# A list schedule made inside the kernel sets the order of four engines behind the first product; loads of pieces and packs on SyncE's queue

## The chip, the cores and the metric

The kernel runs on one core of a Trainium2 chip. The metric is the device time of one execution in microseconds, the median of several runs. TensorE (PE) multiplies, VectorE (DVE), ScalarE (ACT) and GpSimd (POOL) do the elementwise work, SyncE (SP) only issues DMAs. Each engine works through its own list of instructions in order and waits on semaphores for the others.

## The reference

Attention in 8 heads over 8 sequences of 576 tokens, four heads with a window of 32 keys and four with 32 keys at a distance of 4; then a gated feed-forward layer over all 4608 tokens. Inputs and outputs are float32.

```python
scores = scale * np.matmul(q, k.transpose(0, 1, 3, 2))
scores = np.where(masks[None, :, :, :], scores, -1000000000.0)
attn = softmax(scores)                       # written out in the reference
x = np.matmul(attn, v) -> (4608, 512)
g = x @ w_gate                               # 512 x 1536
silu = g * (1.0 / (1.0 + np.exp(-g)))
return silu * (x @ w_val) @ w_out            # 1536 x 512
```

## The kernel before

**Number format.** The products run in a shorter float format (float32r), so each operand is split in a high part (rounded) and a low part (the rest); three products, high-high, low-high, high-low, stand for one.

**Tokens.** They come in nine chunks of 512 columns. The first three (`NPLAIN`) are computed plainly; the last six in three double chunks by a seven-product scheme (Strassen's) that saves one product in eight. Attention comes in 38 packs: scores, mask and maximum (`shift`), `exps`, a turn by TensorE (`turn_e`), a copy (`keys`), `results`, `norm`, `turn_y`, and `x_copies`, which puts the result in place as high and low part. A pack's steps A, B and C are hung into the feed-forward work by a table of slots (`attend`).

**The ramp.** An item is one 128-row slice f of the hidden layer for one chunk: gate product into bank bg (12 matmuls), tanh (`act_tanh`), `dve_u`, value product into bank bv (12), `dve_h`, `h_hi` (rounding, ACT, L537), `h_lo` (low part, POOL, L542), and one item later the out product into bank bo (12, L549), whose last four matmuls need the low part. The first six items have 256 columns (f = 0, 1, 2 for either half of chunk 0), the others 512; items 6 to 14 are f = 3 to 11 of chunk 0, which is when the weights are needed first.

**Weights.** The 24 units of weights arrive as 64-bit numbers (768 KB each, L234, five raw buffers). Each passes five steps, called E, T, B, H and L in the code (`STAGES`): E (ACT, L244) and T (ACT L265 or DVE L268) bring the halves into place, B (DVE, L275 or L278) joins them, H (ACT, L286) rounds, L (POOL, L290) makes the low part. A raw buffer takes its next load when B is done. Units 2f and 2f+1 serve slice f: the gate product needs 2f, the value product both, the out product 2f+1.

**Pieces.** For the last stage the weights are needed in other combinations. They are written to a scratch tensor in DRAM: plain ones straight from the units (`plain_parts`, 54 writes of 256 KB, L692), sums made on DVE and ACT (`mix_stage`, 72 writes, L735). In the last stage 63 pieces of 512 KB are loaded three times (`ask`, POOL's queue, L764) into a ring of seven; a piece serves 12 matmuls (L836). `h_split` (L826, and L797 on POOL or DVE by turns) splits the hidden tiles there, `out_done` stores results (SP, L886).

**Order.** All engines but SP are ordered by hand (`manual_schedule`): instructions run in the order in which the Python code emits them. `unit_first`, `unit_second` and `unit_third` emit the steps of units 2t+2 and 2t+3 at fixed places of item t; `mixing` spreads the 54 mixing stages from item 11 (`W_ITEMS`) on. SP's DMAs were placed by the framework, those of the pieces tied behind the last weight load or mix write (`issue_after`). Pack loads (L347, L354) are issued on ACT's queue behind the exp of the pack before.

## Time and profile before

| what | value |
|---|---|
| time, median of 3 runs (lowest, highest) | 981.69 us (980.54, 985.24) |
| profiled execution, its time | 981.86 us |
| profiled execution, its span | 979.8 us |
| TensorE busy / its weight loads | 926.6 us (95%) / 754.2 us (77%) |
| DVE / ACT / POOL busy | 661.5 (68%) / 386.1 (39%) / 351.8 us (36%) |
| DMA | 204.8 MB, mean 209 GB/s |
| chain that ended last | 68% TensorE, 11% DVE, 4% issue, 3% POOL |

Matmul times are modelled ends and overlap a little; the distance from start to start is the pace. Names are those of the program with buffer numbers left out: bg, bv and bo are the banks of gate, value and out product, `two` that of attention, at_float, at_float32r and at_int are tiles of those types.

### The profile page before, as it was taken

The page shows a single profiled execution, that of the slowest core. Times are in us where ns is not written, and L with a number is a line of the kernel's source. Part 1 is how long each engine was busy: PE and PEld are TensorE (multiplying, and loading weights), DVE is VectorE, ACT ScalarE, POOL GpSimd, SP SyncE. Part 2 cuts the span into 40 slices and gives each one's busy share as a digit, 9 for nine tenths or more (in the row PEclk, how much of TensorE's full clock was granted, in tenths as well). Part 3 has the DMA queues.
Part 4 walks back from the last instruction along what each step waited for, and adds up shares of the span by engine and source line. Part 5 has one row for each costly group of instructions (what it writes and reads, how often), then busy time and mean ns, then how long its engine had stood idle before and what let it go on. Part 6 is the DMA issues. An engine that isn't in the chain of part 4 may idle for free.

```text
span 979.8 us, 20720 instructions
## 1 busy us (share of the span) xinstructions
PE 926.6 (95%) x8701; PEld 754.2 (77%) x8701; DVE 661.5 (68%) x974; ACT 386.1 (39%) x611; POOL 351.8 (36%) x371
## 2 busy tenths in 40 slices
PE   6576988999999999999999989999999999999998
PEld 4475766888888788788788768888888788888886
DVE  4444654665677768876578994767679965465882
ACT  3445453332323233434334443334344533333352
POOL 2334444212211121332324474233244653334582
PEclk7778999999999999999999999999999999999999
DMA  9546523465546577787777577878765596665573
GB/s 356 186 174 207 176 66 111 161 212 197 197 159 229 183 251 255 249 274 238 218 235 237 171 219 231 279 218 264 252 219 171 168 293 207 193 193 173 179 251 108
DMA packets 73964, 204.78 MB, mean 209 GB/s; under 512 B 7440, under 2 KB 21392, under 8 KB 73872
## 3 DMA queue, kind: packets, MB, share of 16 engines
q0 software_dynamic: 27216, 99.10, 33.5%
q1 hardware_dynamic: 36720, 65.98, 19.1%
q10 hardware_dynamic: 9936, 38.39, 11.3%
q8 instruction: 68, 1.11, 0.5%
q14 instruction: 24, 0.20, 0.1%
HBM read 160.97 MB, written 42.47 MB: 208 GB/s over the span
## 4 chain that ended last, share of the span: by engine, by line
PE 68%; DVE 11%; issue 4%; POOL 3%; ACT 2%; DMA 1%; ACTq 0%; POOLq 0%; DVEq 0%
PE bo L836 26%; PE bg L836 10%; PE bv L836 9%; PE bo L549 6%; PE bg L503 6%; PE bv L503 6%; DVE at_float L797 3%; DVE at_float32r L797 2%; PE two L420 2%; PE two L374 2%; POOL at_float32r L797 1%; PE two L406 1%; POOL at_float32r L290 1%; DMA at_float<-qkb 1%; DVE at_float L397 0%
## 5 line engine op out<-in xcount | busy, mean ns | idle before, releaser
L836 PE MATMUL bo<-at_float32r 128*128 128x512 f32 x1296 | 310.3, 392 | 4.9 <-DVE at_float32r L797 4.6
L836 PEld LDWEIGHTS bo<-at_float32r 128*128 128x128 f32 x1296 | 241.4, 188 | 58.1 <-DVE at_float32r L797 5.9
L764 POOL DMA_DIRECT2D at_float32r<-pieces x189 | 103.7, 549 | 267.3 <-PE bo L836 164.7
L797 DVE TENSOR_TENSOR at_float<-bo,at_float 128x512 f32<-128x512 f32 x168 | 113.5, 687 | 99.9 <-ACT at_float L841 53.5
L503 PE MATMUL bg<-at_float32r,at_float32r 128*128 128x512 f32 (+1 forms) x468 | 119.3, 407 | 16.2 <-ACT at_float32r L286 9.3
L836 PE MATMUL bg<-at_float32r 128*128 128x512 f32 x486 | 130.1, 393 | 1.6 <-DVE at_float32r L797 0.8
L836 PE MATMUL bv<-at_float32r 128*128 128x512 f32 x486 | 128.9, 391 | 0.0
L549 PE MATMUL bo<-at_float32r,at_float32r 128*128 128x512 f32 (+1 forms) x468 | 112.4, 388 | 16.7 <-POOL at_float32r L542 16.7
L542 POOL TENSOR_TENSOR at_float32r<-at_float,at_float32r 128x512 fp32r<-128x512 f32 (+1 forms) x39 | 50.6, 1297 | 206.5 <-PE bo L549 126.9
L797 DVE TENSOR_TENSOR at_float32r<-at_float,at_float32r 128x512 fp32r<-128x512 f32 (+1 forms) x84 | 97.3, 1185 | 39.0 <-ACT at_float32r L826 23.6
L503 PEld LDWEIGHTS bg<-at_float32r,at_float32r 128*128 128x128 f32 x468 | 91.3, 210 | 36.2 <-ACT at_float32r L286 10.0
L549 PEld LDWEIGHTS bo<-at_float32r,at_float32r 128*128 128x128 f32 x468 | 84.9, 195 | 35.9 <-POOL at_float32r L542 18.8
L503 PE MATMUL bv<-at_float32r,at_float32r 128*128 128x512 f32 (+1 forms) x468 | 109.8, 385 | 1.5 <-DVE at_float L532 1.5
L836 PEld LDWEIGHTS bg<-at_float32r 128*128 128x128 f32 x486 | 90.3, 188 | 22.2 <-DVE at_float32r L797 1.7
L836 PEld LDWEIGHTS bv<-at_float32r 128*128 128x128 f32 x486 | 90.7, 188 | 19.4
L826 ACT CAST at_float32r<-at_float 128x512 fp32r<-128x512 f32 x126 | 75.0, 622 | 75.0 <-DVE at_float L797 26.9
L797 POOL TENSOR_TENSOR at_float32r<-at_float,at_float32r 128x512 fp32r<-128x512 f32 x63 | 89.5, 1423 | 36.6 <-ACT at_float32r L826 35.8
L503 PEld LDWEIGHTS bv<-at_float32r,at_float32r 128*128 128x128 f32 x468 | 84.9, 196 | 18.2 <-DVE at_float L532 1.8
L862 ACT ACTIVATE at_float<-at_float 128x512 f32<-128x512 f32 x72 | 45.6, 633 | 92.8 <-DVE at_float L797 92.7
L527 DVE SCALAR_TENSOR_TENSOR at_float<-at_float,bg 128x512 f32<-128x512 f32 (+1 forms) x39 | 25.2, 646 | 71.3 <-ACT at_float L522 71.3
L841 ACT COPY at_float<-bg 128x512 f32<-128x512 f32 x63 | 37.1, 588 | 72.2 <-PE bg L836 72.1
L864 DVE SCALAR_TENSOR_TENSOR at_float<-at_float,at_float 128x512 f32<-128x512 f32 x72 | 54.6, 759 | 11.7 <-ACT at_float L862 11.7
(70 smaller groups left out, 944.5 us busy)
## 6 DMA issues: line engine op xcount, KB each, us to landing
at_float32r<-pieces POOLq DMA_DIRECT2D x189, 512.0 KB, 4.6
pieces<-at_float32r SPq DMA_DIRECT2D x126, 256.0 KB, 3.5
at_float<-qkb ACTq DMA_DIRECT2D x32, 576.0 KB, 5.8
at_float<-vb ACTq DMA_DIRECT2D x34, 520.0 KB, 4.6
at_int<-w SPq DMA_DIRECT2D x19, 768.0 KB, 4.3
out<-at_float SPq DMA_DIRECT2D x36, 256.0 KB, 4.6
at_int<-w SPq DMA_DIRECT2D x10, 384.0 KB, 6.7
at_float<-vb SPq DMA_DIRECT2D x8, 260.0 KB, 5.7
```

What stands on the lines that cost most here:

```text
L374: nc.tensor.matmul(out=two[BQ * j:BQ * j + BQ, i, SA + BU * g:SA + BU * g + BU], lhsT=t[r, q:q + BQ], rhs=t[r, k + 1:k + BK], start=not ma ...
L503: nc.tensor.matmul(out=(bank_g, bank_v)[which][:, it.cols], lhsT=wcol(it.f, o, wl), rhs=(x_lo if xl else x_hi)[it.ci % 2][1 - j // 2][:, j ...
L527: last["h"] = nc.vector.scalar_tensor_tensor(out=t, in0=t, scalar=1.0, in1=bank_g[:, it.cols], op0=ALU.add, op1=ALU.mult)
L542: nc.gpsimd.tensor_tensor(out=hl, in0=it.h[0], in1=it.h[1], op=ALU.subtract)
L549: nc.tensor.matmul(out=bank_o[j][:, it.cols], lhsT=wcol(f, 2 * DM + P * j, low), rhs=x, start=f == it.cols.start == low == 0 and x is hh, ...
L764: nc.gpsimd.dma_start(out=taken[asked], in_=pieces[asked % NPIECE])
L797: engine.tensor_tensor(out=out, in0=a, in1=b, op=op)
L826: nc.scalar.copy(out=o[:, 0], in_=src)
L836: nc.tensor.matmul(out=bank, lhsT=w, rhs=x, start=first and n == 0 and t in FRESH, stop=last and n == len(ops) - 1, skip_group_check=True)
L841: nc.scalar.copy(out=kept[KEPT[t]][r], in_=banks[0][r][:, :CS])
L862: nc.scalar.activation(out=f, in_=g, func=AF.Tanh, scale=0.5)
L864: nc.vector.scalar_tensor_tensor(out=f, in0=f, scalar=1.0, in1=g, op0=ALU.add, op1=ALU.mult)
```

## The change

`Desk` stands between the code and the engines. Up to the first product of the feed-forward layer it passes every call on. From `nc.keep` on it records calls with what they read and write, and `nc.issue` at the end orders all of them by a list schedule: each engine takes, among the instructions whose inputs are ready on a modelled clock, the one with the longest way to the end, or waits a little for a longer one. Costs are a constant and a slope for each engine; DMAs go through one modelled pipe of 373 bytes/ns with 2 us to land. TensorE's instructions keep their written order (`spine`). SP is ordered by hand now too. Loads of pieces and packs go to SP's queue. The steps of the units are emitted at the item that needs them (`units`) and mixing from item 15, but the schedule decides when they are issued. No computation is added or taken away.

```diff
+class Desk:
+    COST = {"vector": (155, 1.035), "scalar": (170, 0.86), "gpsimd": (400, 1.75)}
+    OVERLAP, AFTER = {"vector": 80, "scalar": 80}, {"tensor": 180, "sync": 0}
+    LANDING, RATE = 2000, 373
...
+        for k in range(n - 1, -1, -1):
+            e, _, _, cost, later, _, _ = kept[k]
+            way[k] = cost + later + max((way[m] for m in after[k]), default=0)
+            if e == "tensor":
+                if last is not None:
+                    way[k] = max(way[k], cost + way[last])
+                last = k
...
+        spine = [k for k in range(n) if kept[k][0] == "tensor"][::-1]
...
+        def begin(k):
+            e, _, _, _, _, both, _ = kept[k]
+            return max(free[e], ready[k], lock if both else 0)
+
+        while len(order) < n:
+            best = None
+            if spine and not left[spine[-1]]:
+                best = begin(spine[-1]), spine[-1]
+            now = free["tensor"] + (way[spine[-1]] if spine else 0)
+            for e in self.ENGINES[1:]:
+                x = [(begin(k), -way[k], k) for k in queue[e]]
+                if not x:
+                    continue
+                soon = min(x)
+                take = soon
+                for y in sorted(x, key=lambda y: y[1]):
+                    if y[1] >= soon[1]:
+                        break
+                    if y[0] <= soon[0] or soon[0] + kept[soon[2]][3] > max(y[0], now + y[1]):
+                        take = y
+                        break
+                if best is None or take[0] < best[0]:
+                    best = take[0], take[2]
...
+        for k in order:
+            kept[k][1]()
...
-    nc = tc.nc
+    nc = Desk(tc.nc)
...
-    by_hand = tc.manual_schedule(engines={et.PE, et.DVE, et.Activation, et.Pool})
+    by_hand = tc.manual_schedule(engines={et.PE, et.DVE, et.Activation, et.Pool, et.SP})
...
+    nc.keep(dict(tensor=16000, vector=18000, scalar=18000, gpsimd=18000, sync=8000))
...
-                        load_v(m, later, nc.scalar)
+                        load_v(m, later, nc.sync)
...
-                        load_qk(m + 1, later, nc.scalar)
+                        load_qk(m + 1, later, nc.sync)
...
-            nc.gpsimd.dma_start(out=taken[asked], in_=pieces[asked % NPIECE])
+            nc.sync.dma_start(out=taken[asked].bitcast(F32), in_=pieces[asked % NPIECE])
...
-    W_ITEMS = NF - 1
+    W_ITEMS = HALVED + NF
...
+    def units(t):
+        for u in (2 * t, 2 * t + 1):
+            for c in STAGES:
+                if done[c] == u:
+                    w_one(c)
...
+        if it.ci == 0:
+            units(it.f)
         gv_mm(it, 0)
...
+    nc.issue()
+    by_hand.__exit__(None, None, None)
```

The first place is ACT at the start of the ramp, around unit 2 (raw tile 323, joined in tile 493, in the change 444) and pack 2's exp (tile 140). Before:

```order
L286 CAST at_1536_float32r<-at_776_int_346 128x768
L522 ACTIVATE at_512_float_453<-bg 128x256
L402 ACTIVATE at_512_float_140<-at_512_float_140 128x8x63
L244 ACTIVATE at_1536_int_323<-at_1536_int_323 128x768
L265 ACTIVATE at_1536_int_323<-at_1536_int_323 128x768
L537 CAST at_512_float32r<-at_512_float_453 128x256
L286 CAST at_1536_float32r<-at_776_int_493 128x768
L244 ACTIVATE at_1536_int_326<-at_1536_int_326 128x768
```

The same place in the change (every instruction behind the first product has the line of the recorded call, L239):

```order
L223 CAST at_1536_float32r<-at_776_int_346 128x768
L239 ACTIVATE at_1536_int_323<-at_1536_int_323 128x768 x2
L239 ACTIVATE at_512_float_441<-bg 128x256
L239 CAST at_1536_float32r<-at_776_int_444 128x768
L239 ACTIVATE at_512_float_140<-at_512_float_140 128x8x63
L239 ACTIVATE at_1536_int_326<-at_1536_int_326 128x768
L239 COPY at_512_float_240<-two 128x512
L239 CAST at_512_float32r<-at_512_float_441 128x256
```

E and T of unit 2 have moved ahead of the first tanh, and its H ahead of the exp; the rounding of the hidden tile has moved behind.

The second place is POOL from item 2 to item 4. Low parts of the hidden tile go to tile 10616; the tiles of units 6 to 11 are 29400, 30936, 32472, 34008, 35544 and 37080. Before:

```order
L542 TENSOR_TENSOR at10616_512_float32r_512<-at8568_512_float32_453,at9592_512_float32r_510 128x256
L473 TENSOR_TENSOR at19160_1024_float32r_67<-at7304_512_float32_349,at17112_1024_float32r_63 128x2x4x64
L290 TENSOR_TENSOR at29400_1536_float32r_76<-at53976_776_int32_337,at29400_1536_float32r_76 128x768
L290 TENSOR_TENSOR at30936_1536_float32r_77<-at54752_776_int32_346,at30936_1536_float32r_77 128x768
L290 TENSOR_TENSOR at32472_1536_float32r_78<-at55528_776_int32_493,at32472_1536_float32r_78 128x768
L290 TENSOR_TENSOR at34008_1536_float32r_79<-at53976_776_int32_337,at34008_1536_float32r_79 128x768
L542 TENSOR_TENSOR at10616_512_float32r_512<-at9080_512_float32_539,at10104_512_float32r_644 128x256
```

In the change:

```order
L239 TENSOR_TENSOR at19160_1024_float32r_67<-at7304_512_float32_349,at17112_1024_float32r_63 128x2x4x64
L239 TENSOR_TENSOR at10616_512_float32r_443<-at8568_512_float32_441,at9592_512_float32r_442 128x256
L239 TENSOR_TENSOR at29400_1536_float32r_76<-at53976_776_int32_337,at29400_1536_float32r_76 128x768
L239 TENSOR_TENSOR at30936_1536_float32r_77<-at54752_776_int32_346,at30936_1536_float32r_77 128x768
L239 TENSOR_TENSOR at10616_512_float32r_443<-at9080_512_float32_445,at10104_512_float32r_446 128x256
L239 TENSOR_TENSOR at32472_1536_float32r_78<-at55528_776_int32_444,at32472_1536_float32r_78 128x768
```

The low part of item 3 has two units ahead of it instead of four.

The third place is SP's queue behind the load of unit 6. Before, the loads of units 7 to 23 followed each other with nothing between. In the change (raw tiles 14264, 50904 and 52440 are units 7, 8 and 9; 616 and 1896 are pack 4):

```order
L239 DMA pieces_57<-at20184_1536_float32r_70 128x2x256
L239 DMA at616_1280_float32_119<-qkb 128x1152
L239 DMA at14264_1536_int32_323<-w 128x1536
L239 DMA pieces_57<-at23256_1536_float32r_72 128x2x256
L239 DMA at1896_1040_float32_125<-vb 128x1040
L239 DMA at50904_1536_int32_326<-w 128x1536
L239 DMA pieces_57<-at24792_1536_float32r_73 128x2x256 x2
L239 DMA at52440_1536_int32_333<-w 128x1536
```

Writes of plain pieces and the loads of packs have come between the loads of units.

## Rows read from the trace of the kernel before

**Rows 1.** The page's slices: TensorE's busy tenths in 40 equal slices.
```profile
PE   6576988999999999999999989999999999999998
```

**Rows 2.** Stretches: length, busy us (instructions) of each engine, TensorE's clock, DMA share, GB/s.
```profile
22.00:85.00 63.00, 42.62 (x649) 39.08 (x642) 31.47 (x48) 28.50 (x44) 24.41 (x18) 0.75 0.56 193
85.00:185.00 100.00, 86.51 (x730) 69.21 (x731) 57.91 (x79) 44.44 (x63) 39.86 (x25) 0.95 0.40 135
...
160.00:540.00 380.00, 378.59 (x4104) 306.95 (x4103) 270.01 (x438) 132.97 (x204) 91.17 (x96) 1.00 0.65 217
540.00:600.00 60.00, 54.99 (x361) 43.93 (x360) 50.55 (x58) 28.62 (x48) 36.23 (x37) 1.00 0.66 203
600.00:960.00 360.00, 358.47 (x2739) 293.83 (x2738) 253.19 (x352) 146.91 (x247) 155.71 (x187) 1.00 0.71 219
```

**Rows 3.** TensorE's waits, 20 to 160 us: total, times, longest.
```profile
PE bo L549 <- POOL at_float32r L542: 16.7, 6, 4.4
PE bg L503 <- ACT at_float32r L286: 7.4, 2, 4.3
```

**Rows 4.** TensorE in order of time: start, us, instructions [idle before, releaser].
```profile
30.03 3.04 PE L503 MATMUL bg<-at_float32r,at_float32r 128*128 128x256 f32 x12 [3.12 <-ACT at_float32r L286]
...
37.18 1.58 PE L503 MATMUL bv<-at_float32r,at_float32r 128*128 128x256 f32 x12
...
44.53 2.08 PE L503 MATMUL bg<-at_float32r,at_float32r 128*128 128x256 f32 x8 [4.26 <-ACT at_float32r L286]
...
60.22 0.78 PE L503 MATMUL bg<-at_float32r,at_float32r 128*128 128x256 f32 x4 [3.94 <-ACT at_float32r L471]
...
76.44 1.22 PE L549 MATMUL bo<-at_float32r,at_float32r 128*128 128x256 f32 x4 [4.38 <-POOL at_float32r L542]
77.47 2.76 PE L503 MATMUL bg<-at_float32r,at_float32r 128*128 128x256 f32 x12
...
85.45 2.89 PE L503 MATMUL bg<-at_float32r,at_float32r 128*128 128x512 f32 x12
...
98.14 4.50 PE L503 MATMUL bg<-at_float32r,at_float32r 128*128 128x512 f32 x12
102.48 2.89 PE L503 MATMUL bv<-at_float32r,at_float32r 128*128 128x512 f32 x12
...
184.71 2.96 PE L503 MATMUL bg<-at_float32r,at_float32r 128*128 128x512 f32 x12
```

**Rows 5.** The same view of ACT, DVE and POOL, single instructions.
```profile
25.78 0.89 ACT L244 ACTIVATE at_int<-at_int 128x768 f32<-128x768 f32 x1
...
29.16 0.83 ACT L286 CAST at_float32r<-at_int 128x768 fp32r<-128x768 f32 x1
...
27.46 0.96 DVE L275 SCALAR_TENSOR_TENSOR at_int<-at_int 128x768 int32<-128x768 int32 x1 [2.31 <-ACT at_int L265]
...
140.87 1.93 DVE L278 SCALAR_TENSOR_TENSOR at_int<-at_int 128x768 int32<-128x768 int32 x1
...
75.66 0.73 POOL L542 TENSOR_TENSOR at_float32r<-at_float,at_float32r 128x256 fp32r<-128x256 f32 x1
```

**Rows 6.** DMA rate in 40 slices of 0 to 28 us; its mean, 167.2 to 170.2.
```profile
GB/s 0 0 43 147 398 405 407 369 344 400 404 410 410 401 413 401 373 392 404 396 404 371 386 388 410 382 395 405 405 390 396 399 407 388 426 426 426 418 404 325
...
DMA packets 649, 1.10 MB, mean 367 GB/s; under 512 B 63, under 2 KB 167, under 8 KB 648
```

**Rows 7.** SP's longest wait; POOL's piece loads (page); their landing (page).
```profile
SPq L886 <- DVE at_float L797: 402.6, 24, 137.1
...
L764 POOL DMA_DIRECT2D at_float32r<-pieces x189 | 103.7, 549 | 267.3 <-PE bo L836 164.7
...
at_float32r<-pieces POOLq DMA_DIRECT2D x189, 512.0 KB, 4.6
```

**Rows 8.** TensorE's waits, 165 to 980 us.
```profile
PE bo L836 <- DVE at_float32r L797: 4.6, 3, 2.3
...
PE two L374 <- DMA at_float<-qkb: 0.5, 1, 0.5
```

More of the change, by code (lines that the diff above doesn't have):

```diff
@@ L166, in attention_moe @@
     assert M_RAW + 2 * WU * NRAW <= M_X0
-    origin = -(-nc.sbuf_base // 64) * 64
+    origin = -(-tc.nc.sbuf_base // 64) * 64
     named = {}
@@ L178, in at @@
             k = n * 4 // mybir.dt.size(dt)
-            named[key] = nc.alloc_sbuf_tensor_at(f"at{o}_{n}_{dt.name}", [P, k], dt, offset=origin + 4 * o).ap()
+            named[key] = tc.nc.alloc_sbuf_tensor_at(f"at{o}_{n}_{dt.name}", [P, k], dt, offset=origin + 4 * o).ap()
         return named[key]
@@ L233, in w_load @@
         for k in range(parts):
-            last["w"] = nc.sync.dma_start(out=t[:, n * k:n * k + n], in_=w[u // 2, u % 2].bitcast(I32)[:, n * k:n * k + n])
+            nc.sync.dma_start(out=t[:, n * k:n * k + n], in_=w[u // 2, u % 2].bitcast(I32)[:, n * k:n * k + n])
         t = t.rearrange("p (n t) -> p n t", t=2)
@@ L472, in x_copy @@
         else:
-            nc.gpsimd.tensor_tensor(out=xl, in0=src, in1=xh, op=ALU.subtract)
+          nc.gpsimd.tensor_tensor(out=xl, in0=src, in1=xh, op=ALU.subtract)
     clear = set()
@@ L526, in dve_u @@
         t = it.h[0]
-        last["h"] = nc.vector.scalar_tensor_tensor(out=t, in0=t, scalar=1.0, in1=bank_g[:, it.cols],
+        nc.vector.scalar_tensor_tensor(out=t, in0=t, scalar=1.0, in1=bank_g[:, it.cols],
                                                    op0=ALU.add, op1=ALU.mult)
@@ L531, in dve_h @@
         t = it.h[0]
-        last["h"] = nc.vector.scalar_tensor_tensor(out=t, in0=t, scalar=0.5, in1=bank_v[:, it.cols],
+        nc.vector.scalar_tensor_tensor(out=t, in0=t, scalar=0.5, in1=bank_v[:, it.cols],
                                                    op0=ALU.mult, op1=ALU.mult)
@@ L734, in mix_out @@
             p, o = piece_at(i, which, product)
-            last["w"] = nc.sync.dma_start(out=pieces[p, :, o:o + 4 * P], in_=t[:, k].rearrange("p l c -> p (l c)"))
+            nc.sync.dma_start(out=pieces[p, :, o:o + 4 * P], in_=t[:, k].rearrange("p l c -> p (l c)"))
     mixed = 0
@@ L746, in mix_stage @@
             (mix_parts, mix_sums, mix_low)[stage](n)
-            with tc.issue_after(last["w"].ins):
-                if stage == 0:
-                    plain_parts(*divmod(n, 3))
-                elif stage == 2:
-                    mix_out(n)
+            if stage == 0:
+                plain_parts(*divmod(n, 3))
+            elif stage == 2:
+                mix_out(n)
     taken = {}
@@ L920, in attention_moe @@
         attend(3 * t)
-        unit_first(t)
         mixing(t, 0)
@@ L930, in attention_moe @@
         attend(3 * t + 1)
-        unit_second(t)
-        unit_third(t)
         if late:
@@ L944, in attention_moe @@
                 x_step(n)
-    by_hand.__exit__(None, None, None)
     for ci in range(NC):
```

127 lines of the change are left out of this document (117 added, 10 removed).

## The prediction

> **What bounds the kernel now.** The busy shares by slice came first: TensorE fills every slice but the first eight or so [rows 1]. Between 600 and 960 us it is busy 358.5 of 360, between 160 and 540 it is busy 378.6 of 380 [rows 2]. Nothing that reorders the other engines can shorten those stretches, because TensorE's own instructions and their order stay. What can go is in two places. From 22 to 185 us TensorE is idle 20.4 + 13.5 = 33.9 us, with a mean clock of 0.75 and 0.95; from 540 to 600 it is idle 5.0 us [rows 2]. The waits name the releasers: in the ramp it waits most for the low part of the hidden tile (POOL, L542) and for the rounded weights (ACT, L286) [rows 3], later for DVE's split of the hidden tiles (L797) [rows 8].
>
> Is the ramp short of throughput? DVE is busy 89 of 163 us there, ACT 73, POOL 64 [rows 2]. DMA is not full either: the mean is 193 and 135 GB/s, while from 3 to 28 us it runs at about 400 [rows 2, 6]. So the ramp is bound by order. The rows show how. Unit 2's E step stands behind pack 2's exp on ACT and starts at 25.78; so B runs on DVE at 27.46, H on ACT at 29.16, and the gate product of item 1 starts at 30.03 [rows 4, 5]. The low part of item 3 stands behind four weight units on POOL and runs at 75.66; the out product gets its last four matmuls at 76.44 after 4.38 us of waiting [rows 4, 5].
>
> A wait of that size costs twice. Behind it the clock is at its lower level (1.2 of 2.4 GHz) for some 4 us: the 12 matmuls of a 512-column gate took 4.50 us at 98.14 and 2.89 at 102.48, those of 256 columns 2.76 at 77.47 and 1.58 at 37.18 [rows 4]. These durations overlap; pitches from start to start are 4.3 and 2.7, and 2.7 and 1.44.
>
> **Part 1, the ramp's order.** I walk the new order through the first items with durations of the rows and of their kinds (E, T 0.8 us apart, H 0.75, B 0.96, L 1.75, low part 0.73). On ACT unit 2's E and T now stand ahead of the first tanh and its H ahead of pack 2's exp. Its load is there by about 21, B follows pack 2's masking at 23.7, H ends at 25.6, L at 27.4. The exp ends at 26.7 (0.8 later than now), the turning products at 27.8, and item 1's gate starts at 27.8, not 30.0. Its value product needs unit 3: H 32.8, L 34.5, in time. The next step that holds TensorE is pack 3's exp, ending at 36.9; the gate of item 2 starts at 37.5 where it now starts at 44.53. Pack 3's strided x is split by 45.8, where the gate of item 3 now waits at 60.22 for it [rows 4]; I leave 0.9 us of wait, and 0.75 for pack 4's exp. From 47.3 come eight groups of 12 at 1.44 plus 1.4 for a pack: item 6, the first of 512 columns, starts at 60.2, rounded up to 61. It now starts at 85.45. **That is 24.4 us**, about 13 of them waits and 11 clock. It supposes the full clock from about 33 us on.
>
> From 85.45 to the first product of the second chunk at 184.71 [rows 4] there are 13.5 us of idle and three gates at the lower level, 3 x 1.6 = 4.8, with 0.3 for another: **18.6 us**. These go if each weight unit is ready when its item comes. An item of 512 columns takes three groups of 2.78, 8.4 us; its two units cost POOL 3.5 plus 1.3 for the low part, ACT 4.9 with tanh and rounding, DVE 4.3: half of the time. The longest things that can now stand ahead of the low part are one B, one H and one L, 3.5 us; with the chain's own 2.6 that is below the 8.3 us between value product and out product.
>
> I take back **5 us** for what the walk can't see. A B step on DVE at 140.87 took 1.93 us, where its kind takes 0.96 [rows 5]: 1 us more, and I let that reach TensorE in five of the nine full items, since packed engines meet more often than waiting ones. The Trainium skill has a rule that speaks against packing them (page "SBUF — State Buffer", section "Who interferes with whom"): DVE instructions with two inputs in SBUF and GpSimd's take one port pair for a whole instruction, and the other stands still. The 1.93 us agrees with it.
>
> **Part 2, weights and pieces on one queue.** SP's queue now carries, between the unit loads, the pack loads that were on ACT's queue and the plain pieces that were written from 137 us on. Up to the last unit's load I count in the order 24 units (18.9 MB), nine packs (9.7) and 42 piece writes (11.0): 39.6 MB. At 400 GB/s, the rate of the first 28 us [rows 6], that is 99 us; the last unit's item comes at 61 + 8 x 8.4 + 6 for three packs = 134 and needs it some 6 us before. Piece writes alone ran at about 367 GB/s [rows 6], which gives 108. Hidden, by 20 us, in either case: 0 us. The Trainium skill ("DMA: Bandwidth & Descriptors", Specifications) gives about 358 GB/s as HBM's limit for a core; that would be 111 us and leave the sum as it is, and the trace's 400 is above it.
>
> **Part 3, the 189 piece loads move from POOL to SP.** POOL loses 103.7 us of issuing, 549 ns each, and the waits for TensorE that stood ahead of its splits, 267 us [rows 7]. POOL isn't the bound in these stages, so by itself that is 0 us; but between 540 and 600 the splits that TensorE waited 4.6 us for [rows 8] are shared by POOL and DVE. The new order takes what TensorE needs first. Bounds: all 5.0 us, or none; I take 3. Against it, pack loads now share a queue with pieces and stores: TensorE's longest wait for a pack after 165 us is 0.5 [rows 8], and with some 30 packs to come I add **2**. Sum of this part: -1. ACT loses the 68 issues of the packs; it is busy 133 of 380 us where most of them lie [rows 2], so that is 0.
>
> **Sum.** The profiled execution took 981.86 us (span 979.8), 0.2 above the median of 981.69. 981.9 - 24.4 - 18.6 + 5 - 1 = **943 us**.
>
> **Rivals.**
> *Lower clock stays through the small items.* The mean was 0.75 from 22 to 85 [rows 2], and my walk leaves four gaps near 1 us. Then 14 groups of 256 columns between 33 and 61 cost 2.7, not 1.44: 17.6 more, **961**. For it: the stretch before 60 has hardly any full-clock group. Against: the product at 37.18 ran at full clock between two long gaps [rows 4]. 0.12.
>
> *The one queue paces the ramp.* A unit load waits behind pieces that wait for POOL, and eight transfers in flight are the most that the order lets be open. At 260 GB/s for 39.6 MB the last unit lands at 152, is ready at 158 and not 128: 30 us late, **about 970**. For it: no row shows loads and writes mixed on one queue. Against: the rows of either kind are above 360. 0.10.
>
> *Nearly everything is recovered.* Idle 33.9, some 10 of lower clock before 85 (half of 42.6 us of work at half speed) and 5 after it, and 5 at 540: **927 to 932**. 0.10.
>
> *Slower: SP stands at a store.* In the hand order SP waited 402.6 us, up to 137 us at once, in front of the result stores of the last stage [rows 7]; nothing of haste was behind them. Now 189 piece loads are. A piece is wanted six pieces after its slot comes free, 6 x 2.8 = 16.8 us, and a load lands in 4.6 [rows 7], so nothing happens until SP stands 12 us too long. From there each us counts; if each of the 12 pairs of stores held SP 16 us, 4 x 12 = 48: **991**. The rows of the new order speak against it, as the stores stand among loads of the same time; so a plan that errs by over 12 us is needed. 0.06.
>
> *Nothing comes of it*, since DMA or an engine bounds the ramp in a way that the rows hide: 977 to 985. 0.03. By the order the instructions do move, so that it doesn't do what it says is out.
>
> **How the numbers follow.** My own case, 932 to 955, gets 0.59. The range takes in the lower clock and part of the queue case, and the recovered case but for its end: **930 to 964**, about 8 in 10. A measurement here tells 0.5%, 4.9 us, from no change. Faster: 0.59 + 0.12 + 0.10 + 0.10 = 0.91, less 0.02 for the queue case at its worst, 0.89; same 0.04; slower 0.07.
>
> **What would show it.** Right: TensorE busy over 90% from 30 us on, the second chunk's first gate at 141 to 150, the clock at full from about 35, no wait for L542's work above 1 us. The slices after 185 should look as now. Wrong: the first 512-column gate after 70; waits of the E step for a weight load; gaps with "pieces" as releaser in the last stage. If the ramp ends at 146 and the time isn't below 950, the loss is in the last stage, and SP's waits will tell.

## The result and the profile after

| what | before | after |
|---|---|---|
| time, median (lowest, highest) | 983.05 us (980.54, 985.24) | 924.6 us (924.03, 924.92) |
| ratio, 95% interval | | 0.9405, 0.9379 to 0.9432 |
| profiled execution / its span | 981.86 / 979.8 us | 924.03 / 922.3 us |
| TensorE busy / idle in the span | 926.6 / 53.2 us | 907.4 / 14.9 us |

The forecast was 943 us, from 930 to 964. The direction was right; the gain was 57.8 us between the profiled executions where 38.9 was forecast, and 924.6 lies below the range.

One thing has to be put right ahead of the rest. The section on the kernel before says that all engines but SyncE are ordered by hand. That holds up to the last stage; its six chunks stand behind the end of the hand order, so there the framework placed the instructions. The list orders that stage too.

The page's slices, which answer to [rows 1]:

```profile
PE   6899999999999999999999999999999999999998
...
PEclk7999999999999999999999999999999999999999
```

The stretches of [rows 2], with the same columns (the last one is cut at 900 us, since the span now ends at 922):

```profile
22.00:85.00 63.00, 59.45 (x899) 52.57 (x891) 51.30 (x73) 45.66 (x70) 43.60 (x28) 0.97 1.04 396
85.00:185.00 100.00, 100.00 (x925) 81.15 (x924) 71.90 (x114) 40.70 (x59) 38.09 (x24) 1.00 0.61 213
160.00:540.00 380.00, 380.00 (x3994) 309.44 (x3993) 272.63 (x437) 147.73 (x229) 88.16 (x60) 1.00 0.57 192
540.00:600.00 60.00, 60.00 (x634) 49.25 (x633) 40.61 (x65) 23.13 (x36) 6.67 (x5) 1.00 0.79 258
600.00:900.00 300.00, 300.00 (x2117) 246.87 (x2116) 201.22 (x291) 126.33 (x210) 88.29 (x60) 1.00 0.65 214
```

From 85 to 900 us TensorE never stands still. The same engines that had 31, 29 and 24 us of work between 22 and 85 now have 51, 46 and 44, and the DMA's share went from 0.56 to 1.04 while TensorE's busy time went up. TensorE's waits between 20 and 160 us are these, where [rows 3] had 16.7 and 7.4 (columns: total, times, longest):

```profile
PE two L239 <- DVE at_float L239: 1.6, 1, 1.6
PE two L239 <- ACT at_float L239: 1.5, 2, 0.8
PE bg L239 <- DMA at_float<-qkb: 0.4, 1, 0.4
PE bg L239 <- POOL at_float32r L239: 0.4, 1, 0.4
PE bg L239 <- ACT at_float32r L223: 0.2, 1, 0.2
```

Between 165 and 980 us the view of waits has no row at all, where [rows 8] has 4.6 and 0.5. TensorE in order of time, beside [rows 4] (L223 and L239 are the list's own lines, through which every instruction goes, so places are told by tile and count):

```profile
27.07 1.67 PE L239 MATMUL bg<-at_float32r,at_float32r 128*128 128x256 f32 x12
...
35.41 1.68 PE L239 MATMUL bg<-at_float32r,at_float32r 128*128 128x256 f32 x12
...
43.71 0.50 PE L239 MATMUL bg<-at_float32r,at_float32r 128*128 128x256 f32 x2 [0.35 <-POOL at_float32r L239]
44.91 0.66 PE L239 MATMUL two<-at_bfloat,at_float 128*128 128x128 f32 x4 [0.69 <-ACT at_float L239]
...
58.44 2.92 PE L239 MATMUL bg<-at_float32r,at_float32r 128*128 128x512 f32 x12
...
138.12 2.27 PE L239 MATMUL bg<-at_float32r,at_float32r 128*128 128x512 f32 x9
```

The gate of item 1 at 27.07 already runs at the full clock (1.67 us for 12 matmuls of 256 columns; 3.04 before). The first gate of 512 columns comes at 58.44, the first of the second chunk at 138.12.

**Where the time came from.** Starts of the same matmuls in both traces:

| place | before | after | saved up to here |
|---|---|---|---|
| first 512-column gate | 85.45 | 58.44 | 27.0 |
| second chunk's first gate | 184.71 | 138.12 | 46.6 |
| first double chunk | 410.93 | 362.79 | 48.1 |
| second | 609.59 | 554.67 | 54.9 |
| third | 803.91 | 746.56 | 57.4 |
| end of the span | 979.8 | 922.3 | 57.5 |

So 46.6 us came from the ramp, 1.5 from the rest of the plain chunks, 9.2 from the first two double chunks. The last one took 175.9 and takes 175.7.

### The profile page after: what moved, and what is told of

Its sections match the earlier page's. It is cut to its first block, busy times and chain, and to the rows that moved or that the text cites. A ratio compares the mean times of both kernels' runs of the same rounds, so it can differ in the third digit from the quotient of the medians.

```text
span 922.3 us, 20745 instructions
## 1 busy us (share of the span) xinstructions
PE 907.4 (98%) x8701; PEld 742.7 (81%) x8701; DVE 633.8 (69%) x974; ACT 391.6 (42%) x611; POOL 268.6 (29%) x182
## 4 chain that ended last, share of the span: by engine, by line
PE 95%; DMA 4%; DVE 0%; SPq 0%; ACT 0%; issue 0%; DVEq 0%
PE bo L239 43%; PE bv L239 23%; PE bg L239 22%; PE two L239 7%; DMA at_int<-w 3%; DMA pieces<-at_float32r 1%; DMA at_float<-qkb 1%; DVE at_float L239 0%; SPq L223 0%; PE two L223 0%; PE fs L223 0%; PE fk L223 0%; ACT at_float L239 0%; ACT at_float L223 0%; SPq L239 0%
## 5 line engine op out<-in xcount | busy, mean ns | idle before, releaser
L239 PE MATMUL bo<-at_float32r 128*128 128x512 f32 x1296 | 309.2, 392 | 0.0
L239 PEld LDWEIGHTS bo<-at_float32r 128*128 128x128 f32 x1296 | 241.7, 188 | 51.8 <-ACT at_float L239 0.4
L239 POOL TENSOR_TENSOR at_float32r<-at_float,at_float32r 128x512 fp32r<-128x512 f32 (+1 forms) x112 | 169.1, 1514 | 369.5 <-ACT at_float32r L239 191.6
L239 ACT CAST at_float32r<-at_float 128x512 fp32r<-128x512 f32 (+2 forms) x214 | 148.0, 705 | 160.8 <-DVE at_float L239 85.7
L239 DVE TENSOR_TENSOR at_float<-bo,at_float 128x512 f32<-128x512 f32 x168 | 114.6, 686 | 115.6 <-ACT at_float L239 71.4
L239 DVE TENSOR_TENSOR at_float32r<-at_float,at_float32r 128x512 fp32r<-128x512 f32 (+1 forms) x102 | 106.9, 1063 | 57.2 <-ACT at_float32r L239 47.2
L239 PE MATMUL bg<-at_float32r 128*128 128x512 f32 x486 | 129.0, 392 | 0.0
L239 PE MATMUL bv<-at_float32r 128*128 128x512 f32 x486 | 128.8, 391 | 0.0
L239 ACT ACTIVATE at_float<-at_float 128x512 f32<-128x512 f32 (+1 forms) x108 | 67.7, 630 | 124.4 <-DVE at_float L239 124.2
L239 POOL TENSOR_TENSOR at_float<-at_float,at_float 128x512 f32<-128x512 f32 x36 | 50.2, 1394 | 226.8 <-DVE at_float L239 225.8
L239 PE MATMUL bg<-at_float32r,at_float32r 128*128 128x512 f32 (+1 forms) x468 | 109.8, 383 | 3.8 <-ACT at_float32r L223 2.0
L239 PE MATMUL bv<-at_float32r,at_float32r 128*128 128x512 f32 (+1 forms) x468 | 109.0, 382 | 0.0
L239 PE MATMUL bo<-at_float32r,at_float32r 128*128 128x512 f32 (+1 forms) x468 | 108.6, 380 | 0.1
L239 DVE SCALAR_TENSOR_TENSOR at_float<-at_float,at_float 128x512 f32<-128x512 f32 x144 | 105.0, 730 | 3.8 <-ACT at_float L239 2.9
L239 PEld LDWEIGHTS bv<-at_float32r 128*128 128x128 f32 x486 | 90.7, 188 | 19.2
L239 PEld LDWEIGHTS bg<-at_float32r 128*128 128x128 f32 x486 | 90.6, 188 | 19.1
L239 PEld LDWEIGHTS bg<-at_float32r,at_float32r 128*128 128x128 f32 x468 | 84.0, 192 | 21.5 <-ACT at_float32r L223 2.6
L239 PEld LDWEIGHTS bv<-at_float32r,at_float32r 128*128 128x128 f32 x468 | 83.8, 192 | 16.8 <-POOL at_float32r L239 0.4
L239 PEld LDWEIGHTS bo<-at_float32r,at_float32r 128*128 128x128 f32 x468 | 82.7, 188 | 17.7 <-POOL at_float32r L239 0.3
L239 ACT COPY at_float<-bg 128x512 f32<-128x512 f32 x63 | 37.1, 589 | 84.9 <-PE bg L239 84.7
L239 DVE TENSOR_TENSOR at_float<-at_float,at_float 128x504 f32<-128x504 f32 (+2 forms) x84 | 69.5, 838 | 1.4 <-ACT at_float L239 1.2
L239 ACT COPY at_float<-bv 128x512 f32<-128x512 f32 x63 | 37.1, 589 | 34.6 <-PE bv L239 33.9
```

The costliest lines, as they stand in the source:

```text
L239: self.kept.append([engine, lambda: f(*a, **k), sorted(m for m in after if m >= 0), cost, later, both, start])
```

## The experiments

The theory on trial is that the order does it all: nobody stands in front of TensorE's next operand any more, and queues matter only by how they shift that order. The rivals are that the queues (POOL freed of its loads, packs off ACT) bring the gain, that a full DMA or collisions between DVE and POOL hold something back, and that the gain behind 185 us follows from the ramp. Each run has its own kernel before beside it on the same chip (medians 982.8 to 984.0). The first four ran on one chip, the other eight on a second one; there the changed kernel was measured once more. One thing helps in reading the starts below. TensorE's first matmul of the list comes at 16.23 us in both traces above. In the runs below that are made from the changed kernel it comes at 16.67 to 17.33 (at 16.16 in the changed kernel's second trace), so 0.4 to 1.1 us of a later start lies ahead of the list.

**The changed kernel again** gave 924.96 us (924.38 to 926.43), ratio 0.941 (0.9396 to 0.9424).

> The changed kernel once more, as a measure beside the others of this call: 924 to 927 if chips differ by as little as the kernel before showed between them (983.1 and 984.0).

### Is it the queue of the pieces?

```diff
-            nc.sync.dma_start(out=taken[asked].bitcast(F32), in_=pieces[asked % NPIECE])
+            nc.gpsimd.dma_start(out=taken[asked], in_=pieces[asked % NPIECE])
```

> The change with the 189 piece loads back on POOL's queue, everything still ordered by the list schedule. The stretch behind the plain chunks became 8 us of idle shorter than before. Theory A, the order of the instructions did it: 924 to 926, TensorE's waits behind 140 us below 1 us. Theory B, it is POOL's freedom from 104 us of issuing and from waiting for TensorE ahead of its splits: most of the 8 us come back, 929 to 933, with waits for at_float32r tiles in the last stage.

924.72 us (924.19 to 926.47), 0.9409 (0.9388 to 0.9431); the double chunks start at 363.38, 555.27 and 747.15, each 0.6 later than in the changed kernel, and so is the list's first matmul (16.80). With the 189 loads back on POOL nothing is lost. Under the list the move of the piece loads is worth nothing, as the prediction had it.

### Is it the queue of the packs?

```diff
-                        load_v(m, later, nc.sync)
+                        load_v(m, later, nc.scalar)
...
-                        load_qk(m + 1, later, nc.sync)
+                        load_qk(m + 1, later, nc.scalar)
```

> The change with the 68 pack loads back on ACT's queue. Theory A (two queues share the same engines, order is all): 924 to 926. Theory B (one queue makes packs wait behind pieces or weights; I had charged 2 us for it): 922 to 924. Theory C (ACT's instructions stand behind the issues, and a load that waits holds ACT): 926 to 930.

930.45 us (929.56 to 931.77), 0.9465 (0.9447 to 0.9484): 5.7 more than the run above on the same chip (4.9 between the profiled executions). All of it is in the ramp: the first 512-column gate starts at 64.26, 5.2 later than in the run above, 0.4 of that ahead of the list, and from there the two kernels keep step (double chunks at 368.6, 560.5, 752.4). TensorE there, and ACT's row that it waits for (pack 3's x being rounded; the same row of the changed kernel last):

```profile
46.17 1.22 PE L239 MATMUL bg<-at_float32r,at_float32r 128*128 128x256 f32 x4 [2.28 <-ACT at_float32r L239]
```
```profile
39.21 1.72 ACT L239 ACTIVATE at_int<-at_int 128x768 f32<-128x768 f32 x2
...
45.02 1.10 ACT L239 CAST at_float32r<-at_float 128x512 fp32r<-128x512 f32 x1 [0.95 <-DVE at_float L239]
```
```profile
40.87 1.13 ACT L239 CAST at_float32r<-at_float 128x512 fp32r<-128x512 f32 x1 [0.95 <-DVE at_float L239]
```

ACT is busy 15.2 and 12.1 of 20 us in the two stretches around this (20 to 40, 40 to 60); in the changed kernel it is 15.1 and 13.6. So ACT has no lack of time. With the issues in its list the schedule comes out in another order, the rounding comes 4.1 us later (1.0 of it ahead of the list), and the wait of 2.28 is followed by a mean clock of 0.83 between 40 and 60 us, where it was 1.00. The rounding itself stands behind DVE in both kernels (0.95); which step ahead of it moved first is not shown.

### Does the list matter behind the ramp?

Two kernels end the list ahead of the last stage, which the framework orders as it did before; one loads the pieces on POOL's queue, the other on SP's.

```diff
+    nc.issue()
+    by_hand.__exit__(None, None, None)
+
     for ci in range(NC):
...
-    nc.issue()
-    by_hand.__exit__(None, None, None)
```

> The list schedule only up to the last stage; the last stage is left to the framework as before, its piece loads on POOL as before. Packs stay on SP. So the ramp is new, the last stage old. If the gain behind the plain chunks belongs to the last stage's order and queues: 924.6 + 8 to 10 = 932 to 935, with the waits of before between 540 and 600 there again some 50 us earlier. If the ramp alone carried the gain in time and pace: 925 to 927.

> As the run with the list schedule only up to the last stage, but with the piece loads of the last stage on SP. Theory A (order): as that run, 932 to 935. Theory B (POOL freed): 924 to 928. The slower rival of the prediction (SP stands at a result store with piece loads behind it) would show here, where no schedule places the stores: over 940, with TensorE waiting for piece loads.

932.21 us (931.96 to 932.41), 0.9482 (0.9466 to 0.9498), with the pieces on POOL; 931.07 (930.94 to 931.64), 0.9472 (0.9456 to 0.9488), on SP. The waits of [rows 8] are back in the first, to the tenth (TensorE's waits, 165 to 980 us):

```profile
PE bo L223 <- DVE at_float32r L223: 4.6, 3, 2.3
```

Its first two double chunks take 197.4 and 194.0, together 7.6 us more than the 191.9 and 191.9 under the list. That is the whole difference to the run with the pieces on POOL above, 7.5 us. With the pieces on SP they take 195.3 and 194.0, and the same wait comes to 4.1 us; so there, too, most of the loss is in the order. TensorE waits for no piece load, so no store holds the loads up; that rival was to show above 940.

The reverse is the kernel before, by hand through the plain chunks, with the list for the last stage alone. The first try had the pieces on SP's queue:

```diff
+    by_list = tc.manual_schedule(engines={et.PE, et.DVE, et.Activation, et.Pool, et.SP})
+    by_list.__enter__()
+    nc.keep(dict.fromkeys(nc.ENGINES, 411000))
     for ci in range(NC):
...
+    nc.issue()
+    by_list.__exit__(None, None, None)
```

> The kernel before, its order by hand kept through the plain chunks; only the last stage is issued by the list, with the pieces and the last stage's packs on SP's queue. Theory 'order of the last stage': the pair of chunks loses the 7 to 8 us that went missing when the list left the last stage alone, and about 1 more for short waits of TensorE: 972 to 976, ramp as before (first 512-column gate at 85, second chunk at 185), double chunks 192 long instead of 194 to 199. Rival 'the late gain is a gift of the ramp' (the last stage only goes faster because something set up in the ramp is different): 981 to 985. Rival 'SP stands at a store': above 985.

982.37 us (976.27 to 983.92), 0.9975 (0.9956 to 0.9993): by its time the rival was right. Two of its ten executions took 976.3 and 978.0, though, the others 981.7 to 983.9, and the trace of one of these others (982.2) says otherwise. Its first two double chunks take 193.9 and 192.1, 7.0 us less than before, but the first starts at 417.91, 7.0 late. This is TensorE ahead of it, within a run of 64 like matmuls of attention:

```profile
369.38 0.74 PE L223 MATMUL two<-at_float 64*32 64x63 f32 x51 [0.26 <-DMA at_float<-qkb]
374.49 0.46 PE L223 MATMUL two<-at_float 64*32 64x63 f32 x13 [4.37 <-issue]
```

It stands for 4.37 us behind the 51st matmul, waiting for nothing that the profile shows ("issue"). From 370 to 374.4 the DMA's share is 0.98, and these queues moved packets between 369.5 and 374.5 (packets, MB, share):

```profile
q1 hardware_dynamic: 826, 1.73, 93.1%
q8 instruction: 1, 0.02, 1.2%
```

One packet of instructions came through in that time, among the piece writes; the view does not say for which engine. So the second try left the piece loads on POOL's queue and nothing else was changed:

```diff
-            nc.sync.dma_start(out=taken[asked].bitcast(F32), in_=pieces[asked % NPIECE])
+            nc.gpsimd.dma_start(out=taken[asked], in_=pieces[asked % NPIECE])
```

> As the run before it that gave only the last stage to the list, but with the piece loads left on POOL's queue, as in the kernel before. There TensorE stood 4.37 us at 374 us in the middle of a run of like matmuls, waiting for nothing that the profile shows, while the DMA was full with piece writes and piece loads; the two double chunks behind it were 7.0 us shorter than in the kernel before. Theory 'order of the last stage, and the stall is a transfer of instructions behind a full DMA': without the piece loads in that stretch the stall goes or shrinks below 1.5, the double chunks keep their 192 us, and the time is 975 to 978. Rival 'the list brings nothing there by itself': 981 to 985 with no stall to excuse it.

975.52 us (974.24 to 975.8), 0.9919 (0.9905 to 0.9934): 7.3 us below the kernel before. TensorE's waits between 165 and 985 us are down to

```profile
PE bg L239 <- ACT at_float L239: 1.4, 1, 1.4
PE two L223 <- DMA at_float<-qkb: 0.5, 2, 0.3
```

and the first two double chunks take 193.6 and 191.9. The gain of the last stage does not need the ramp's, and the two ways of measuring it agree: 7.5 taken away, 7.3 put in.

### Does SP stand at a store?

The kernel before, with the first edit above turned round: the piece loads on SP's queue, the order as it was.

> The kernel before with one change: the 189 piece loads are issued on SP's queue, not POOL's; the order is what it was. Theory 'the order does it all': POOL's 103.7 us of issuing bounded nothing, so 981 to 984, no change, as the pair with and without it under the list showed 0 and 1 us. Rival of the prediction 'SP stands at a store': SP waits up to 137 us in front of the result stores in this order, and here nothing puts the loads among them in the right order, so above 990, with pieces as TensorE's or DVE's releaser in the last stage. Rival 'POOL freed is worth something by itself': 976 to 980.

987.49 us (981.12 to 990.87), 1.0028 (1.0006 to 1.005), a small loss that scatters: three of its ten executions took 981.1 to 983.7, the other seven 987.0 to 990.9. The profiled one (983.7) is of the three. It shows no trace of the rival in the last stage: the double chunks take 198.7 and 193.9, as before. What it has more is a wait for a pack at 369.79, at the place of the stall above:

```profile
369.79 0.85 PE L374 MATMUL two<-at_float 64*32 64x63 f32 x64 [1.78 <-DMA at_float<-qkb]
```

On SP's queue the first piece loads start at 350.87, in the kernel before at 375.07, since there they stand behind POOL's waits for TensorE; and the DMA runs at a share of 0.90 and 0.96 from 350 to 370, where it was 0.77 and 0.66. So neither the theory's 981 to 984 nor the rival's place holds. In this trace early piece loads fill the DMA where mix writes and a pack are under way; that the seven longer executions lose their time there is not shown.

### Is the full DMA of the ramp hidden?

The plain piece writes are held until 110 us on the list's modelled clock.

```diff
-        start = max([-1 - m for m in after if m < 0], default=0)
+        start = max([-1 - m for m in after if m < 0] + [self.hold])
```

> The changed kernel with the writes of the plain pieces held back until a modelled 110 us, so that the first 100 us of the DMA carry weights and packs alone. Theory 'a full DMA is hidden': all 16 DMA engines are busy from 20 to 80 us in the changed kernel, yet TensorE is busy 20.00 of 20 us from 60 on, so taking load away gives 924 to 925.5, and the DMA is no longer full there. Rival 'the pieces slow the ramp's first 45 us', where the chain of waits goes over two transfers of 9.9 and 6.5 us: 920 to 923, with the first 512-column gate at 55 to 57 instead of 58.4.

928.14 us (926.56 to 930.55), 0.9432 (0.9411 to 0.9452), against 0.941 (0.9396 to 0.9424): at best nothing won. From 40 to 80 us the DMA fell from about 395 to 282 GB/s, and the 768 KB units landed in 6.4 us instead of 9.3 (medians of the whole run). Still the first 512-column gate starts at 59.00, not 55 to 57. That is 42.2 us behind the list's first matmul, as in the changed kernel. The rival is out: with the writes gone and the loads landing sooner, TensorE comes to that gate at the same pace. Of the 2 us more at the first double chunk (364.84) 0.6 lie ahead of the list, and 0.7 are a wait for a pack's exp that this order has at 56 to 85 us.

### What does one wait cost?

At one item of the second chunk the low part of the hidden tile is made eight times more on POOL.

```diff
+            for _ in range(8 if t == 20 else 0):
+                h_lo(it)
```

> The changed kernel with one stall put in: at one item of the plain chunks the low part of the hidden tile is made nine times over on POOL instead of once, some 5.8 us more there, of which part is slack. It measures what a wait of TensorE costs as a whole. Theory 'a wait costs twice': after a gap of several us the next 512-column gate runs at the lower clock, 4.3 instead of 2.78, so the time is 924.6 plus the gap seen plus about 1.5 to 1.8 us. Rival 'a wait costs its length': 924.6 plus the gap seen. If the gap is under 1 us the run decides nothing.

933.43 us (932.33 to 934.03), 0.9482 (0.9468 to 0.9496). TensorE at the place, and the mean clock of stretches of 2 us (the column ahead of the last two):

```profile
200.35 2.14 PE L239 MATMUL bo<-at_float32r,at_float32r 128*128 128x512 f32 x8
207.63 2.08 PE L239 MATMUL bo<-at_float32r,at_float32r 128*128 128x512 f32 x4 [5.14 <-POOL at_float32r L239]
209.50 4.45 PE L239 MATMUL bg<-at_float32r,at_float32r 128*128 128x512 f32 x12
213.79 2.96 PE L239 MATMUL bv<-at_float32r,at_float32r 128*128 128x512 f32 x12
```
```profile
204.00:206.00 2.00, 0.00 (x0) 0.00 (x0) 2.00 (x2) 1.31 (x2) 1.92 (x2) 0.99 0.11 46
206.00:208.00 2.00, 0.37 (x1) 0.37 (x2) 1.93 (x3) 0.00 (x0) 1.92 (x3) 0.50 0.00 0
...
210.00:212.00 2.00, 2.00 (x6) 1.58 (x5) 0.89 (x2) 1.04 (x1) 1.17 (x1) 0.50 0.00 0
212.00:214.00 2.00, 2.00 (x8) 1.60 (x7) 0.36 (x1) 0.00 (x0) 0.00 (x0) 0.80 0.39 143
```

From this out product to the next value product the changed kernel takes 2.90 + 2.78 = 5.68 us; here it is 213.79 - 200.35 = 13.44, 7.8 more for a gap of 5.14. The rest, 2.6, is work at the lower clock (0.50): the four matmuls of the out product and the twelve of the next gate. The theory's sum, 924.6 + 5.1 + 1.8, is 931.5; it left out the four matmuls, 0.9, and 0.7 was late already ahead of the gap (200.35, where the changed kernel has 199.63).

### Which part of the list does it?

First the priority: the ready instruction that comes first in the program, in place of the one with the longest way to the end.

```diff
+        way = [n - k for k in range(n)]
```

> The changed kernel, whose list takes among the ready instructions not the one with the longest way to the end but the one that comes first in the program. It asks whether the gain lies in the priority or only in letting nobody stand behind an instruction that is not ready. Theory 'readiness is the main thing': most of the 58 us stay, 925 to 935, the loss in the ramp, where the engines have a backlog; from 185 us on no difference. Rival 'the longest way is the main thing': 945 or more, with waits for POOL's low part of the hidden tile again.

944.4 us (942.95 to 944.62), 0.9602 (0.9588 to 0.9617): 19.4 more than the changed kernel on that chip, so 38.4 of the 57.8 us come without the longest way and 19.4 need it. That is between the two forecasts, and the loss isn't in the ramp alone: 8.1 us there (first 512-column gate at 66.52; 1.1 of it ahead of the list), 11.6 in the first two double chunks (196.9 and 198.7, with 192.0 each in the changed kernel's second trace). The waits that the rival named, for POOL's low part of the hidden tile ahead of an out product, are not there; gate products wait, 6.1 us for POOL and 5.5 for ACT in all. Two things are not taken apart: the rule by which an engine waits for a longer instruction reads the same numbers, so it changed too, and the 38.4 hold what the new places of emission (`units`, mixing from item 15) bring.

Then the modelled lock: the list holds DVE's two-input instructions and POOL's apart (`both`). Here it doesn't.

```diff
-            both = engine == "gpsimd" or engine == "vector" and len(ins) == 2 and all(x.space != bass.MemoryType.PSUM for x in ins)
+            both = False
```

> The changed kernel with a list that knows nothing of DVE's two-input instructions and POOL's standing in each other's way: the modelled lock is off, all else as it is. It asks about the 5 us that the prediction took back for such collisions and that did not show. Theory 'the engines have room, collisions never reached TensorE': 924 to 927. Rival 'the list avoids them, and that is why they cost nothing': 928 to 934, with more and longer collisions (POOL's and DVE's mean durations up in the ramp) and waits for POOL's or DVE's splits.

936.79 us (936.09 to 937.52), 0.9526 (0.951 to 0.9542), 11.8 more and past the rival's own figure: 6.4 in the ramp up to the first 512-column gate (at 64.82; 0.6 of it ahead of the list), 6.5 in the first two double chunks (196.4 and 194.1). In between, nothing is lost. This is TensorE without the lock, from that gate to the first one of the second chunk, and a stretch of it with the columns of [rows 2]:

```profile
64.82 2.92 PE L239 MATMUL bg<-at_float32r,at_float32r 128*128 128x512 f32 x12
...
144.52 2.94 PE L239 MATMUL bg<-at_float32r,at_float32r 128*128 128x512 f32 x12
```
```profile
85.00:140.00 55.00, 55.00 (x490) 44.95 (x489) 38.96 (x52) 29.38 (x41) 31.64 (x18) 1.00 0.75 259
```

The way takes 79.70 us; in the changed kernel it takes 138.12 - 58.44 = 79.68. So through the nine full items the collisions do not reach TensorE with the lock in the model or without.

The B step on DVE in its two forms, and POOL's low part of 256 columns, from 20 to 100 us (busy, mean ns, idle before); the changed kernel first, then the one without the lock:

```profile
L239 DVE SCALAR_TENSOR_TENSOR at_int<-at_int,at_int 128x768 int32<-128x768 int32 x9 | 12.3, 1364 | 0.0
L239 DVE SCALAR_TENSOR_TENSOR at_int<-at_int 128x768 int32<-128x768 int32 x10 | 11.8, 1176 | 0.7 <-issue 0.7
...
L239 POOL TENSOR_TENSOR at_float32r<-at_float,at_float32r 128x256 fp32r<-128x256 f32 x6 | 7.1, 1188 | 3.0 <-ACT at_float32r L239 3.0
```
```profile
L239 DVE SCALAR_TENSOR_TENSOR at_int<-at_int,at_int 128x768 int32<-128x768 int32 x9 | 13.0, 1440 | 0.1
L239 DVE SCALAR_TENSOR_TENSOR at_int<-at_int 128x768 int32<-128x768 int32 x9 | 10.7, 1193 | 5.9 <-issue 2.2 <-POOL at_float32r L239 2.0 <-ACT at_int L239 1.6
...
L239 POOL TENSOR_TENSOR at_float32r<-at_float,at_float32r 128x256 fp32r<-128x256 f32 x6 | 6.6, 1095 | 4.7 <-ACT at_float32r L239 4.7
```

Both forms together, B takes a mean of 1.11 us in the kernel before, 1.27 in the changed one and 1.32 without the lock; POOL's low part takes 0.73, 1.19 and 1.10. So in the packed ramp these instructions get longer with the lock in the model or without, and there the model makes little difference to their lengths. In the last stage it makes one. DVE's splits of 512 columns behind 165 us, in the kernel before, in the changed one and without the lock, and a row of the latter's TensorE:

```profile
L797 DVE TENSOR_TENSOR at_float32r<-at_float,at_float32r 128x512 fp32r<-128x512 f32 x63 | 69.4, 1129 | 23.7 <-ACT at_float32r L826 23.6
```
```profile
L239 DVE TENSOR_TENSOR at_float32r<-at_float,at_float32r 128x512 fp32r<-128x512 f32 x63 | 56.8, 914 | 33.7 <-ACT at_float32r L239 33.5
```
```profile
L239 DVE TENSOR_TENSOR at_float32r<-at_float,at_float32r 128x512 fp32r<-128x512 f32 x63 | 63.4, 1025 | 24.5 <-ACT at_float32r L239 24.5
```
```profile
538.29 1.52 PE L239 MATMUL bo<-at_float32r 128*128 128x512 f32 x5 [2.50 <-DVE at_float32r L239]
```

The last row is a wait of 2.50 us for such a split, in the stretch where before waited, too.

One rival is left for both prices. Other edits that only shift the list's input lost time as well (5.7 us with the packs on ACT's queue, some 3 with the writes held back). How much of the 19.4 and the 11.8 any other order would have lost, no run tests.

## Why the prediction came out low in gain

**The walk through the ramp: right.** The forecast starts were 27.8, 37.5, 45.8 (the gate that waits for pack 3) and 61; they are 27.07, 35.41, 43.71 and 58.44, and of the two short waits forecast there, 0.9 and 0.75, there came 0.35 and 0.69. The second chunk's gate was to come 43 us earlier by the walk and came 46.6 earlier. Of the 3.6 that it is short, 2.6 lie ahead of the first 512-column gate.

**The 5 us taken back for collisions: wrong.** The 1.93 us of [rows 5] was a true sign, though "its kind takes 0.96" came from a single row: B took 1.11 on average in the kernel before, and rose to 1.27. The step that failed is "I let that reach TensorE in five of the nine full items". It cost nothing: from 58 us on TensorE waits for nothing, and without the modelled lock it goes through these items in the same time (79.70 and 79.68 us). So it was not the list's knowledge of the lock that kept collisions away from TensorE there; the engines have room, as the prediction's own count of an item said ("half of the time"). What the kernel without it lost, 11.8 us, it lost in other places, in the ramp's small items and in the last stage. "SBUF — State Buffer", section "Who interferes with whom", in the Trainium skill gives the reason why such a model is worth building: a lock on one shared port pair. The durations here agree with it (the splits of the last stage take 914 ns with the lock in the model and 1025 without); the price depends on the order, and the page can't give it.

**Part 3, -1 us behind 185: the largest miss.** It was 10.9. The step that failed is "Nothing that reorders the other engines can shorten those stretches". The idle time of the three stretches of [rows 2] behind 160 us is 1.4 + 5.0 + 1.5 = 7.9, and all of it went; the sum had 3 of the 5.0 and nothing of the rest. The list for the last stage alone gave 7.3 us. A wait also delays TensorE by somewhat more than its idle time, since modelled ends overlap. The two longest that the kernel before has behind 165 us:

```profile
575.62 5.76 PE L836 MATMUL bo<-at_float32r 128*128 128x512 f32 x24 [1.15 <-DVE at_float32r L797]
583.67 1.43 PE L836 MATMUL bo<-at_float32r 128*128 128x512 f32 x5 [2.29 <-DVE at_float32r L797]
584.93 0.84 PE L836 MATMUL bg<-at_float32r 128*128 128x512 f32 x3
```

From 575.62 to 583.67 are 8.05 us, and 24 of these matmuls take 5.46 from start to start: 2.6 lost for a gap of 2.29. By the same count seven late waits with 7.0 us of idle time cost 8.4. This is not the price of the injected wait (7.8 for 5.14). Behind that one the clock was at 0.50; here it stayed at 1.00 ([rows 2], 540 to 600), so "costs twice", which the prediction had said of the ramp, does not hold for these waits. The other 2.5 of the 10.9 no run takes apart.

**The +2 for packs on one queue: wrong in sign.** There is no wait for a pack behind 165 us. And the step "ACT loses the 68 issues of the packs", put at 0, was costed by ACT's busy share. Put back on ACT's queue they cost 5.7 us, in the ramp, where ACT still has time to spare; as far as the trace shows it is by way of another order.

Put together: 3.6 for the walk, 5 for the take-back and 9.9 for Part 3 are 18.5. The sum stood at 942.9 and the profiled execution took 924.0; of the 18.9 between them 0.3 lies outside of the span.

**Part 2: right in size, and hidden.** The DMA is full from 20 to about 96 us, where 99 to 108 had been reckoned for the traffic up to the last unit's load; from 20 to 100:

```profile
DMA packets 15664, 30.99 MB, mean 387 GB/s; under 512 B 1154, under 2 KB 11720, under 8 KB 15653
```

The 387 GB/s are above the Trainium skill's 358 ("DMA: Bandwidth & Descriptors", Specifications), as the 400 of [rows 6] were. TensorE waits 0.4 us for DMA from 20 us on.

**The rivals.** Lower clock: out, the mean is 1.00 from 40 us on. One queue that paces the ramp: out, with the DMA full and TensorE at 59.45 of 63. SP at a store: out in the changed kernel, where SP waits at most 7.2 us for DVE's results (before 137.1, [rows 7]), and not seen in the one trace of the kernel before with the piece loads on SP. "Nearly everything is recovered", 927 to 932, was the right case and had 0.10; with the 7.9 idle us behind 160 in place of 5 its sum is 33.9 + 10 + 5 + 7.9 = 56.8, and that gives 925. That it comes so near is in part luck: its 48.9 up to 185 us are 2.3 more than the 46.6 measured, and its 7.9 behind are 3.0 less than the 10.9. **What would show it** pointed the right way: the second chunk's gate at 138 instead of 141 to 150, a gate at the full clock at 27, and the slices after 185 not "as now" but full, which was the sign of the missed 10.9.

## What to carry to other kernels

When every engine has slack and the one that bounds still waits, the order is the thing to change. A list that takes what is ready and has the longest way to the end was 19 us better here than the same list in program order, and 12 us better with a model of which instructions lock each other out than without, in one pair of runs each. Count idle microseconds, not the busy share, also where the stretch looks full: two stretches of together 740 us, 99.6% busy, and one of 60 beside them held 7.9 us of idle time, and 10.9 us were to be had behind the ramp. A wait costs a little more than its length, and half as much again where the clock falls behind it (7.8 us for 5.14).

## What was not expected of the hardware

- **TensorE can stand still with nothing to wait for.** In one kernel it stood 4.37 us within a run of like matmuls with no wait, while the DMA's share was 0.98 and one packet of 0.02 MB went through a queue of instructions. With the piece loads on POOL's queue the stall was gone in the one trace that was taken, and all four executions took 974.2 to 975.8 us. The Trainium skill ("Runtime: NRT & Kernel Launch", section "Instruction fetch mechanics") says that a sequencer fetches its instructions in blocks of 16 KB through a DMA queue of its own and that the cost is mostly hidden. The trace agrees with the block; that the block was late because data stood ahead of it is what the pair of runs suggests, and no row proves it. In the changed kernel the DMA was full from 20 to 96 us, and TensorE has no gap of this kind longer than 1.0 in the whole run.
- **The units took twice as long to land.** With the DMA full and weights, packs and pieces on one queue, units of 768 KB landed in 9.3 us, where the kernel before has 4.3. With the plain writes held back it was 6.4, and that kernel was no faster.
- **The lower clock outlasts a gap.** The injected gap ran from about 202.5 to 207.63. The granted clock was 0.99 from 204 to 206, all of it idle, 0.50 from 206 to 212, 0.80 from 212 to 214 and full from 214, so most of the slow time fell on work.
